# Attention and expert routing: the stretch ahead of the experts in a new order, and new clocks for where routing's steps go

## Chip, cores, metric

The kernel runs on one core of one Trainium2 chip. The metric is device time in microseconds (us) of one execution. The time before is the median of three runs, 891.27 us.

## The reference, cut to what matters

Sigmoid attention over 8 batches of 12 heads with 448 positions of width 64 gives x, 3584 tokens of width 768. A gate scores each token for 8 experts; a greedy assignment in order of score gives each expert exactly 448 tokens; each token goes through its expert's two products.

```python
attn = 1.0 / (1.0 + np.exp(-(scale * q @ k.T - np.log(S))))     # B,H,S,D = 8,12,448,64
x = (attn @ v).transpose(0, 2, 1, 3).reshape(B * S, H * D)      # 3584 x 768
logits = x @ w_gate                                             # 3584 x 8
for idx in np.argsort(-logits.flatten()):
    tok, e = idx // E, idx % E
    if assigned[tok] >= 0 or counts[e] >= cap: continue         # cap = 448
    assigned[tok] = e; counts[e] += 1
for e in range(E):
    m = assigned == e
    out[m] = np.maximum(x[m] @ w1[e], 0) @ w2[e]                # 768 -> 1024 -> 768
```

## The kernel before

The program's order is written by hand: each engine runs its instructions in the order in which the Python code emits them, and waits for data and buffers. An instruction that waits holds up everything behind it on its engine.

**Attention.** 48 pairs of heads, one after the other. `scores` makes products on TensorE and the sigmoid on ScalarE; `av` (L452 on) multiplies with v and copies the result from PSUM into `XT[b]` (six slots of 448 columns per batch) with VectorE (L469); for every second pair a rest is added to the slot before (L471). `logits(b, prs)` (L476 on) multiplies `XT` slots with the gate weights into `LE` (L482, L484). For the last batch, slots 0 to 3 go ahead of the last `av`, slots 4 and 5 behind it.

**Ahead of the experts.** `rows(b, c)` transposes 112 tokens of `XT` back (six TensorE transposes, L490), copies them with ScalarE into a buffer `xr` (L492) and writes them to `xs` in DRAM (L493, issued on SP's queue). There are 32 such row blocks, kept in the list `late`. `Router.start` transposes `LE` (L134) into `ML`, the table of scores. Then routing for the first expert runs on TensorE and VectorE; after each step that it yields, `LATE_PER_STEP` = 2 row blocks are emitted (`LATE_KEYS` after the first).

**Routing one expert** (`Router.phase`). `keys` (VectorE) makes a key per token and expert. `search` transposes the keys (L162, TensorE; copy L165, VectorE) and then finds the threshold of the 448th key for all experts in 16 steps: three counting instructions each (L173), a sum over partitions, and a few small ones. For expert 0 the sum is a TensorE product (L185); for the others it is done on VectorE alone. `pick` (L224 on) chooses the expert, `place` (L252, L257, L258) numbers its tokens, and `lists` compares the number's residue `rr` with 0 to 63 in one large VectorE instruction, the one-hot `oh` (L279), from which TensorE makes the list of tokens `idx` (L284, L291, L293).

**The experts.** `moe(kx)` is a generator that yields once per product of 448 columns: 144 for the first layer (L680 to L684, three per tile because each operand is split into a high and a low part) and 144 for the second (L715 to L719); 36 more for expert 0, whose first part is cut in two, and 48 more in the last. The loop at the end of the file drives it. It adds each product's cost (`MM` = 189 ns) to `clock[0]` and decides after each product what else to emit:

- a step of the next expert's routing, when the clock has passed `t_route`. The step yields the time (`T_KEYS`, `T_DVE`, ...) after which the next one follows, to which `SLACK` = 150 is added;
- a chore, at most one per `CHORE_NS` = 1000: the gather of a token block from `xs` (GpSimd's queue, L618), a *turn* of half a gathered block (`xturn`: three TensorE transposes L632 into a PSUM buffer `tp`, ScalarE's copy L635 to `xh`, VectorE's subtraction L636 to `xl`, which frees `tp`), or an `untranspose` of a part of the output (L645 into `tp`, copy L650). There are two `tp` buffers, used in turn. The chores of expert kx + 1 begin when its list is finished (`prepare`), the turns `lag` later.

`stream` loads weights through SP and splits them into `wh` (ScalarE, L596) and `wl` (L598, mostly GpSimd).

## Time and profile before

| | |
|---|---|
| runs | 888.68, 891.27, 891.42 us; median 891.27 |
| the profiled execution | 887.23 us; span from first to last instruction 885.5 us |
| mean granted TensorE clock | 0.984 |
| busy: TensorE, VectorE, ScalarE, GpSimd | 837.8, 531.4, 456.2, 467.4 us |
| attention | 0 to about 274 us of the span |
| ahead of the experts | about 274 to 335 us |
| experts | about 335 us to the end |

In a timeline row the numbers are start and length in us, then engine, line, operation, what it writes and reads, the shape, how many are merged, and in brackets the idle time of the engine before it with what ended it. A TensorE product's length is modelled and reaches beyond the start of the next one; the distance of two starts tells the pace.

### The profile page before, as it was taken

How to read it: one execution, taken by the hardware profiler on the slowest of the kernel's cores; microseconds unless marked ns; L12 is line 12 of the kernel's file. 1: busy time of each engine (PE TensorE's matmuls, PEld its weight loads, DVE VectorE, ACT ScalarE, POOL GpSimd, SP SyncE). 2: the span in 40 equal slices, each digit the busy share in tenths (PEclk: the TensorE clock that was granted, in tenths of full speed). 3: DMA queues.
4: the chain of work that ended last, by engine and by line, in shares of the span. 5: the costliest groups of instructions: out<-in, count | busy, mean ns of one | idle time of the engine just before them, and what ended most of it. 6: DMA issues, size and time to landing. Idle time of an engine off the chain costs nothing.

```text
span 885.5 us, 16232 instructions
## 1 busy us (share of the span) xinstructions
PE 837.8 (95%) x5507; PEld 639.0 (72%) x5507; DVE 531.4 (60%) x2047; ACT 456.2 (52%) x610; POOL 467.4 (53%) x449
## 2 busy tenths in 40 slices
PE   6999999999998729998999999999999999999996
PEld 3455455455555518987988988988888888889996
DVE  4665555555554778958869779779689521421110
ACT  6777777777774724434424424434434434443431
POOL 9645444444400014846864964873883882752651
PEclk9999999999999969999999999999999999999999
DMA  9876666665603945434443542452552542632511
GB/s 172 168 144 127 132 125 123 131 126 120 138 12 100 299 161 153 136 107 161 136 133 117 146 156 75 157 164 95 153 164 70 178 146 72 228 111 72 192 49 63
DMA packets 203507, 117.57 MB, mean 133 GB/s; under 512 B 143936, under 2 KB 193088, under 8 KB 203424
## 3 DMA queue, kind: packets, MB, share of 16 engines
q1 hardware_dynamic: 190688, 83.03, 36.0%
q0 software_dynamic: 10880, 33.28, 11.9%
q8 instruction: 43, 0.70, 0.3%
q10 hardware_dynamic: 1856, 0.23, 0.2%
q14 instruction: 40, 0.33, 0.1%
HBM read 94.47 MB, written 22.02 MB: 132 GB/s over the span
## 4 chain that ended last, share of the span: by engine, by line
PE 77%; DVE 8%; DMA 5%; issue 4%; POOL 3%; ACT 1%; SPq 1%; POOLq 0%; ACTq 0%; DVEq 0%
PE tp L461 13%; PE sc L437 11%; PE sc L682 8%; PE sc L680 8%; PE sc L684 8%; PE sc L717 6%; PE sc L719 6%; PE sc L715 6%; PE tp L467 2%; DMA xs<-xr 2%; DVE r_junk L173 2%; PE sc L447 2%; PE tp L645 2%; DMA xr<-xs,r_idx 2%; PE tp L632 2%
## 5 line engine op out<-in xcount | busy, mean ns | idle before, releaser
L598 POOL TENSOR_TENSOR wl<-wr,wh 128x768 fp32r<-128x768 f32 (+1 forms) x96 | 205.9, 2155 | 134.6 <-ACT wh L596 126.9
L427 ACT ACTIVATE at<-sc,bias 128x896 f32<-128x896 f32 x168 | 161.0, 1006 | 63.1 <-PE sc L447 38.2
L372 POOL DMA_DIRECT2D nkq<-in_q_dram x188 | 118.6, 646 | 111.5 <-DVE kqT L412 104.7
L719 PE MATMUL sc<-hh,wl 128*128 128x448 f32 (+2 forms) x400 | 151.4, 378 | 0.0
L717 PE MATMUL sc<-hl,wh 128*128 128x448 f32 (+2 forms) x400 | 145.4, 364 | 0.1
L684 PE MATMUL sc<-xh,wl 128*128 128x448 f32 (+2 forms) x396 | 145.4, 367 | 0.0
L682 PE MATMUL sc<-xl,wh 128*128 128x448 f32 (+2 forms) x396 | 144.9, 366 | 0.0
L715 PE MATMUL sc<-hh,wh 128*128 128x448 f32 (+2 forms) x400 | 143.9, 360 | 0.0
L680 PE MATMUL sc<-xh,wh 128*128 128x448 f32 (+2 forms) x396 | 143.8, 363 | 0.0
L173 DVE TENSOR_SCALAR_CACHE_REDUCE r_junk<-r_KE,r_T 128x224 bf16<-128x224 f32 x315 | 123.2, 441 | 0.1
L461 PE MATMUL tp<-at,nv 128*64 128x448 f32 x576 | 118.8, 548 | 0.0
L596 ACT ACTIVATE wh<-wr 128x768 fp32r<-128x768 f32 (+1 forms) x112 | 102.0, 939 | 13.2 <-DMA wr<-in_moe_w_dram 13.1
L692 POOL TENSOR_TENSOR hl<-yt,hh 128x896 fp32r<-128x896 f32 x32 | 68.3, 2136 | 44.5 <-ACT yt L691 41.8
L421 DVE TENSOR_TENSOR kqL<-kqT,kqH 128x896 fp32r<-128x896 f32 (+1 forms) x49 | 52.6, 1073 | 58.3 <-ACT kqH L419 58.2
L688 ACT ACTIVATE hh<-sc 128x896 fp32r<-128x896 f32 x32 | 29.5, 920 | 111.0 <-PE sc L684 111.0
L618 POOL DMA_INDIRECT xr<-xs,r_idx x32 | 32.0, 1002 | 97.5 <-ACT wh L596 86.7
L717 PEld LDWEIGHTS sc<-hl,wh 128*128 128x128 f32 x400 | 75.2, 188 | 7.0 <-issue 1.1
L598 DVE TENSOR_TENSOR wl<-wr,wh 128x768 fp32r<-128x768 f32 (+1 forms) x16 | 25.1, 1571 | 91.7 <-ACT wh L596 91.5
L461 PEld LDWEIGHTS tp<-at,nv 128*64 128x64 f32 x576 | 37.1, 136 | 59.1 <-issue 57.9
L682 PEld LDWEIGHTS sc<-xl,wh 128*128 128x128 f32 x396 | 74.5, 188 | 6.3 <-issue 0.5
L715 PEld LDWEIGHTS sc<-hh,wh 128*128 128x128 f32 x400 | 75.6, 189 | 4.4
L680 PEld LDWEIGHTS sc<-xh,wh 128*128 128x128 f32 x396 | 74.7, 189 | 5.5
(156 smaller groups left out, 1323.7 us busy)
## 6 DMA issues: line engine op xcount, KB each, us to landing
wr<-in_moe_w_dram SPq DMA_DIRECT2D x64, 384.0 KB
wr<-in_moe_w_dram SPq DMA_DIRECT2D x48, 512.0 KB
xs<-xr SPq DMA_DIRECT2D x32, 336.0 KB
nkq<-in_k_dram SPq DMA_DIRECT2D x190, 56.0 KB
nkq<-in_q_dram POOLq DMA_DIRECT2D x188, 56.0 KB, 2.6
nv<-in_v_dram SPq DMA_DIRECT2D x92, 96.0 KB
nr<-in_v_dram SPq DMA_DIRECT2D x46, 32.0 KB
xr<-xs,r_idx POOLq DMA_INDIRECT x32, 4.4
```

Source lines behind the costliest of these rows:

```text
L173: nc.vector.tensor_scalar(junk, KE, T[:, i:i + 1].bitcast(F32), None, OP.is_ge, OP.add, accum_out=cnt[:, i:i + 1])
L372: qn.dma_start(t[o:o + 32, n], rws[x])
L427: nc.scalar.activation(a, p[:, :, :S], AF.Sigmoid, bias=bias, scale=1 / math.sqrt(D))
L461: nc.tensor.matmul(p[j * 64:j * 64 + 64, :S], nat["v", b, g][:, h0 + j, c, :], AT[b, pr, c][:, j, :], start=(c == 0), stop=(c == 2 and pr ...
L596: nc.scalar.activation(hi, raw[u], AF.Copy)
L598: eng.tensor_tensor(lo, raw[u], hi.bitcast(F32), OP.subtract)
L680: nc.tensor.matmul(ph[:, f, lo:hi], wh[:, a, fs], xh[:, dd, lo:hi], start=st, stop=False)
L682: nc.tensor.matmul(ph[:, f, lo:hi], wh[:, a, fs], xl[:, dd, lo:hi], start=False, stop=False)
L684: nc.tensor.matmul(ph[:, f, lo:hi], wl[:, a, fs], xh[:, dd, lo:hi], start=False, stop=en)
L715: nc.tensor.matmul(py[:, d2, :w], wh[:, a, dsl], h1, start=st, stop=False)
L717: nc.tensor.matmul(py[:, d2, :w], wh[:, a, dsl], h2, start=False, stop=False)
L719: nc.tensor.matmul(py[:, d2, :w], wl[:, a, dsl], h1, start=False, stop=(j == 1 and a == 3))
```

## The change

It is made in four places.

1. *End of attention.* All six slots of the last batch's logits are made in one go after the loop; the last `XT` copy is made by ScalarE; no row block stands between the logits and `Router.start`.
2. *Ahead of the experts.* The pool with `XT` (`xa`) is opened below the attention's working pools `ld` and `wk`, which are closed first. In their space lie eight `xr` buffers (four before); the row blocks have three PSUM buffers (two before). The experts' PSUM pools `ps_t` and `ps_s` are opened after the row blocks, and the experts' SBUF pools now start on `XT`'s space. `LATE_KEYS` is 3.
3. *The one-hot's input.* For experts 1 to 7 the residue `rr` is written to PSUM as float32, not to SBUF as int16.
4. *The clocks.* `MM` is 206. A second clock `dve[0]` follows VectorE: a routing step adds its cost to it, a turn adds `T_XL`. The next step follows at `dve[0]` + `T_HOP` (150) if it begins on TensorE with what VectorE made, else at `dve[0]` + `T_FEED` (−400). Turns, untransposes and such TensorE beginnings now also advance `clock[0]` (`T_TURN`, `T_BACK`, `T_PE`). Step times are new, the sixteenth search step is emitted together with what follows it, and `lag` runs from 6500 to 17000 instead of 5000 to 14000.

```diff
-XA_BUFS = 4
+XO_BUFS = 8
-LATE_KEYS = 2
-T_KEYS, T_KE, T_STEP, T_DVE, T_KAP, T_PICK, T_TOT, T_OH, T_BT = 3600, 2100, 2050, 2025, 500, 2600, 600, 3800, 600
-SLACK = 150
+LATE_KEYS = 3
+T_KEYS, T_STEP0, T_STEP, T_KAP, T_PICK, T_TOT, T_OH, T_BT = 4850, 3300, 2340, 350, 3000, 700, 4900, 1500
+T_HOP, T_FEED, T_XL, T_TURN, T_BACK, T_PE = 150, -400, 560, 420, 300, 250
...
-            if not pe:
-                yield T_DVE
+            if not pe and st < 15:
+                yield T_STEP if st else T_STEP0, False
...
-        rr = wk.tile([112, 32], I16, name="r_rr")
+        rr = wk.tile([112, 32], I16, name="r_rr") if alone else P[:, 320:352]
...
-            yield T_KEYS
+            yield T_KEYS, True
             yield from self.search(k == 0)
-            yield T_KAP
+            yield T_STEP + T_KAP, True
...
-            nc.vector.tensor_copy(XT[b][:, pr, :], p[:, :S])
+            (nc.scalar.copy if (b, pr) == (B - 1, NP - 1) else nc.vector.tensor_copy)(XT[b][:, pr, :], p[:, :S])
...
-            if old == (B - 1, NP - 2):
-                bg.append(lambda: logits(B - 1, range(NP - 2)))
...
-        logits(B - 1, [NP - 2, NP - 1])
-        late.pop(0)()
+        logits(B - 1, range(NP))
...
         pctx.close()
-        ps_t = ctx.enter_context(tc.tile_pool(name="ps_t", bufs=2, space=PSUM))
-        ps_s = ctx.enter_context(tc.tile_pool(name="ps_s", bufs=2, space=PSUM))
+        lctx.close()
         ps_a = ctx.enter_context(tc.tile_pool(name="ps_a", bufs=2, space=PSUM))
+        xo = actx.enter_context(tc.tile_pool(name="xo", bufs=1))
+        ps_s = actx.enter_context(tc.tile_pool(name="ps_w", bufs=3, space=PSUM))
...
         actx.close()
+        ps_t = ctx.enter_context(tc.tile_pool(name="ps_t", bufs=2, space=PSUM))
+        ps_s = ctx.enter_context(tc.tile_pool(name="ps_s", bufs=2, space=PSUM))
...
 # in xturn:
+            if not wide:
+                clock[0] += T_TURN
+            dve[0] = max(dve[0], clock[0] + 900) + T_XL
...
 # in untranspose:
+            clock[0] += T_BACK
...
-        MM = 189
+        MM = 206
...
-                lag = max(5000, min(14000, start + 40000 - t0))
+                lag = max(6500, min(17000, start + 50000 - t0))
...
                 if t >= t_route:
-                    t_route = t + next(route, 0) + SLACK
+                    cost, hop = next(route, (0, False))
+                    dve[0] = max(dve[0], t) + cost
+                    clock[0] += T_PE if hopped[0] else 0
+                    hopped[0] = hop
+                    t_route = dve[0] + (T_HOP if hop else T_FEED)
```

## The prediction

> **What bounds the kernel now.** I read the page first, then the busy time by stretches, then the timelines of the stretch ahead of the experts and of one expert's turn into the next, then the list of waits.

> ```profile
> span 885.5 us, 16232 instructions
> PE 837.8 (95%) x5507; PEld 639.0 (72%) x5507; DVE 531.4 (60%) x2047; ACT 456.2 (52%) x610; POOL 467.4 (53%) x449
> ...
> 284.00:287.00 3.00, 1.88 (x17) 1.70 (x17) 2.45 (x17) 1.99 (x3) 0.00 (x0) 1.00 0.93 300
> ...
> 350.00:360.00 10.00, 10.00 (x51) 9.28 (x50) 9.44 (x61) 3.19 (x4) 8.42 (x6) 1.00 0.40 107
> ```

> Columns of a stretch: its length, busy time of PE, weight load, VectorE (DVE), ScalarE (ACT) and GpSimd (POOL), granted clock, DMA share, GB/s. TensorE is full except in two kinds of place. Ahead of the experts (274 to 335 us) it waits for VectorE, which runs the first of the searches, while the rows of x leave at 300 GB/s. From 335 us on it is full and VectorE nearly so while a search runs, so there the order of the two queues decides. The profiled execution took 887.23 us (its span and 1.8 around it), 4.0 less than the median 891.27; I sum differences and add them to the median. About 0.3%, 2.7 us, is what a measurement here can tell from no change.

> **Ahead of the experts.**

> ```profile
> 269.51 0.97 PE L482 MATMUL tp<-xt,wgz 128*32 128x112 f32 x32
> 270.42 2.48 PE L461 MATMUL tp<-at,nv 128*64 128x448 f32 x12
> 272.82 0.98 PE L467 MATMUL tp<-at,nr 64*64 64x448 f32 x8
> 275.18 0.59 PE L482 MATMUL tp<-xt,wgz 128*32 128x112 f32 x16 [1.37 <-DVE xt L471]
> 277.55 0.65 PE L134 MATMUL rt<-ident,LE 128*112 128x128 f32 x2 [0.98 <-ACT xr L492]
> ...
> 286.65 0.17 PE L185 MATMUL rt<-r_cnt,c_G 128*128 128x3 bf16 x1 [1.02 <-DVE r_junk L173]
> 288.50 0.16 PE L185 MATMUL rt<-r_cnt,c_G 128*128 128x3 bf16 x1 [0.32 <-DVE r_junk L173]
> 290.35 0.16 PE L185 MATMUL rt<-r_cnt,c_G 128*128 128x3 bf16 x1 [0.19 <-DVE r_junk L173]
> ...
> 316.85 0.16 PE L185 MATMUL rt<-r_cnt,c_G 128*128 128x3 bf16 x1 [1.68 <-DVE r_junk L173]
> ...
> 331.70 0.87 PE L632 MATMUL tp<-ident,xr 128*128 128x128 f32 x3 [5.05 <-DMA xr<-xs,r_idx]
> ...
> 273.88 0.62 DVE L469 COPY xt<-tp 128x448 f32<-128x448 f32 x1 [3.05 <-PE tp L467]
> ```

> (1) All 48 logit products of the last batch come after the last attention products, the first row block after R.start, and ScalarE makes the last XT copy. The 32 products at 269.51 leave the front: attention's end moves up 0.91 (270.42 − 269.51), from 273.8 to 272.9. The copy (0.62 on VectorE) runs beside VectorE's addition instead of ahead of it; both end at about 273.55. The logits' PSUM buffer is the one the copy frees, so the 48 start then, not earlier; 32 cost 0.91 and 16 cost 0.52, so they end at 275.0, not 275.7. LE's addition (0.27) follows, and L134 no longer waits for the row block's ScalarE copy: it starts at about 275.4, not 277.55. I take 2.2 us; bounds 0.7 (the logits alone) and 3.0.

> (2) Search 0 has 16 steps, with two row blocks behind each of the first 14. Undisturbed, a step takes 1.85 us (288.50 to 290.35). From 286.65 to 316.85 are 14 steps in 30.20, 2.16 each, because TensorE stands in front of a row block whose ScalarE copy waits:

> ```profile
> 305.19 1.60 ACT L492 COPY xr<-sc 112x768 f32<-112x768 f32 x2 [1.22 <-DMA xs<-xr]
> ...
> DMA to landing us min/median/max: 3.7/4.4/5.6
> ```

> Eight xr buffers and three of PSUM replace four and two. Will the DMA allow it? At 0.93 busy it moved 300 GB/s, 323 if full, so a block of 0.344 MB needs 1.07 to 1.15 us, against 0.925 asked: over 24 blocks it falls behind by 3.4 to 5.4 us, and four more buffers hold 4 × 1.1 = 4.4. It just about fits. So 14 × (2.16 − 1.85) = 4.3 us; bounds 0 (DMA sets the pace after all) and 4.3.

> The three early row blocks (LATE_KEYS 3) replace the one that stood ahead of R.start: 32 either way. The rest of the chain, pick to first gather, is the same instructions. Moving xa below ld and wk puts the weight buffers on XT's space; they must wait for the last row block on TensorE, and the two search steps left after it (3.7 us) and the pick cover that. The writes to xs end at about 278 + 32 × 1.1 + 2 = 315; the gathers that read them start one landing (4.4) ahead of the first turn, at 331.7 − 4.4 − 6.5 = 321. On SP's queue the first weights stand behind the same 32 writes. This costs nothing, at most 1 us where the weights meet the last writes.

> Ahead of the experts: −6.5 us (−0.7 to −7.5).

> **In the experts.** I counted the emission in both versions, matmul by matmul, with the code's own clocks. The plain pace is 25 matmuls in 5.06 us, 0.2025 each, so MM 189 ran 7% fast and 206 is right.

> ```profile
> 373.83 0.36 PE L719 MATMUL sc<-hh,wl 128*128 128x448 f32 x1
> ...
> 378.89 0.36 PE L715 MATMUL sc<-hh,wh 128*128 128x448 f32 x1
> ...
> 461.18 0.39 PE L162 MATMUL rt<-ident,r_KT 112*128 112x112 f32 x2
> 463.26 0.49 PE L632 MATMUL tp<-ident,xr 128*128 128x128 f32 x3
> 464.81 0.49 PE L632 MATMUL tp<-ident,xr 128*128 128x128 f32 x3
> ...
> 468.72 0.55 PE L632 MATMUL tp<-ident,xr 128*128 128x128 f32 x3 [0.65 <-DVE xl L636]
> ...
> 475.23 0.39 PE L632 MATMUL tp<-ident,xr 64*128 64x64 f32 x3 [0.15 <-DVE xl L636]
> ...
> 463.79 0.49 ACT L635 ACTIVATE xh<-tp 128x384 fp32r<-128x384 f32 x1 [0.32 <-PE tp L632]
> ...
> 461.60 0.39 DVE L165 COPY r_KE<-rt 128x224 f32<-128x224 f32 x1 [0.57 <-PE rt L162]
> ...
> 465.33 0.55 DVE L636 TENSOR_TENSOR xl<-tp,xh 128x384 fp32r<-128x384 f32 x1
> ...
> 468.12 1.01 DVE L636 TENSOR_TENSOR xl<-tp,xh 128x384 fp32r<-128x384 f32 x2
> ...
> 471.38 1.01 DVE L636 TENSOR_TENSOR xl<-tp,xh 128x384 fp32r<-128x384 f32 x2
> ```

> A turn (xturn) needs one of two tp buffers, and the turn two before frees it with VectorE's subtraction L636. If a search step was emitted in between, that subtraction stands behind 2.3 us of VectorE work (468.12 − 465.83; a pair of subtractions takes 1.01). That is the wait at 468.72: TensorE stops, and all its matmuls queue behind the turn.

> Before, turns are 6 matmuls apart (6 × 189 passes CHORE_NS = 1000) and steps 12. Now T_TURN adds 420 to the clock, so 3 × 206 + 420 already passes 1000: turns are 3 matmuls apart. T_XL charges VectorE's clock, but t_route was set when the last step was issued, so the charge moves the next step but one. In expert 1 the count, in matmul numbers: first step (with L162) 246, turns 251, 254, step 255, turns 257, 260, 263, step 265, turns 266, 269, 272. Before: first step 239, turns 248 to 288, four steps in between.

> TensorE from L162 to the last turn, after: 26 × 0.2025 + 7 turns × 0.33 (464.81 − 463.26 less 6 matmuls) + L162 0.26 (461.18 to 463.26 less 9 matmuls) = 7.8 us. VectorE until that turn may start (it needs the sixth subtraction): 0.42 to the key copy, 3.5 for copy and first step (461.60 to 465.33, less some 0.2 that the step lost to POOL's splits), two subtractions 1.0, a step 2.3, two 1.0, 0.6 idle because the fifth turn starts only when the third's buffer is free (0.53 to ScalarE, 0.49 there), 0.55, a step 2.3, 0.5: 12.1 in round numbers. TensorE stands 4.3 us; I take 4.0. The same sum for before: 49 × 0.2025 + 2.3 + 0.26 = 12.5 against 0.42 + 3.5 + 6 × 0.5 + 3 × 2.3 = 13.8, a wait of 1.3; the trace has 14.05 from 461.18 to 475.23, so 1.5. The method holds.

> (3) Experts 1 to 4 turn their successors among search steps; in 5 and 6 the searches are over. After: 4 × 4.0 = 16. Before, this row bounds it:

> ```profile
> PE tp L632 <- DVE xl L636: 3.2, 5, 0.9
> ...
> 405.49 1.01 PE L632 MATMUL tp<-ident,xr 128*128 128x128 f32 x6 [0.85 <-DVE xl L636]
> ...
> 407.21 0.86 PE L632 MATMUL tp<-ident,xr 64*128 64x64 f32 x6 [0.71 <-DVE xl L636]
> ```

> 3.2 less 1.56 at the first turn of experts is 1.6; the brackets leave out some 0.2 to 0.3 of modelled tail at each stall, so I take 3.5. Difference +12.5; bounds 0 (the steps fall clear of the turns) and +14.4.

> (4) Expert 0 to 1: the list is finished at matmul 288 (281 before), the last three gathers stay behind the weight split on POOL, and a search step now falls between the third turn and its predecessors. +1; bounds 0 and +2.5.

> (5) T_KEYS 4850 puts 26 matmuls (5.3 us) instead of 20 (4.1) between the keys and their transposes. T_OH 4900 gives the one-hot 24 instead of 21. Those waits go:

> ```profile
> 648.34 0.38 PE L162 MATMUL rt<-ident,r_KT 112*128 112x112 f32 x2 [0.31 <-DVE r_KT L153]
> ...
> 516.64 1.08 PE L284 MATMUL rt<-r_oh,c_mv 112*32 112x64 f16 x32 [0.28 <-DVE r_oh L279]
> ```

> Four of the first kind (one each for experts 2 to 5) and one of the second: −1.5.

> (6) The residue in PSUM:

> ```profile
> L279 DVE TENSOR_TENSOR r_oh<-c_io,r_rr x8: 1215/1440/3005, 323.7 to 712.7; 112x2048 f16<-112x2048 int16 x8
> ...
> 448.75 0.19 PE L257 MATMUL rt<-r_mk,c_TRI 112*112 112x64 bf16 x1
> ...
> 451.15 3.00 DVE L279 TENSOR_TENSOR r_oh<-c_io,r_rr 112x2048 f16<-112x2048 int16 x1
> ```

> No row has this comparison with an f32 input from PSUM. Operations that do read PSUM in f32 take 0.55 us for 384 elements (465.33) and 0.62 for 448 (273.88), 1.1 ns an element, so 2048 take 2.4. It starts 2.4 after L257 (448.75 to 451.15), 4.8 in all under 24 matmuls, 4.9: hidden, cost nothing. At the 3.00 of the slowest row it would cost 0.5 seven times, 3.5; at the fastest, 1.22, nothing again, and a gain has no way in once TensorE does not wait.

> Everything else in the clocks (T_BACK, T_PE, T_PICK, T_BT, lag) moves work among full TensorE time: nothing.

> Sum in the experts: 12.5 + 1 − 1.5 = +12. Whole: 12 − 6.5 = +5.5, so 891.3 + 5.5 = **897 us**; its own range is 892 to 902.

> **A rule weighed: the clock.**

> ```profile
> 274.00:278.00 4.00, 1.84 (x25) 1.49 (x26) 1.30 (x4) 0.80 (x1) 0.00 (x0) 0.93 0.00 0
> 278.00:281.00 3.00, 3.00 (x16) 2.92 (x15) 2.53 (x6) 1.01 (x2) 0.00 (x0) 0.52 0.39 120
> ...
> 400.00:410.00 10.00, 6.88 (x42) 5.28 (x41) 7.58 (x31) 4.91 (x10) 2.96 (x4) 1.00 0.42 139
> ```

> With TensorE 46% busy over 4 us the clock was halved for 3.4 us behind it; with 69% over 10 us it was not. My stalls of 1.3 to 1.6 us lie between turns and leave TensorE over half busy, so I add nothing; were all four groups and the first turn to halve the clock, 5 × 3.4 / 2 = 8.5 us come on top. [...]

> **The rivals.** *Faster, by the search steps clearing the turns.* If VectorE reaches the subtractions as T_XL means it to, the groups' waits go (−3.5), with +1, −1.5 and −6.5: 891.3 − 10.5 = 881; with some left, 881 to 886. It decides from the point where a group stands less than 2.6 us ((6.5 + 1.5 + 3.5 − 1) / 4). For it speaks the new pace of TensorE's clock; against it the 2.3 us between pairs of subtractions. 0.17.

> *About level:* groups at half my wait: 891 − 2.5 = 889, up to 893. 0.12.

> *The change ahead of the experts does not do what it says:* the writes were 0.93 busy already, so the pace stays 2.16 and only 2.2 is won: 891.3 + 12 − 2.2 = 901. Against it: only 4 blocks in flight at 4.4 us each. 0.08.

> *The clock falls in the stalls:* 897 + 1.7 to 8.5 = 899 to 905. 0.06.

> My forecast has 0.57.

> **How the numbers follow.** Faster than 888.6 holds the first rival and part of the second: 0.20. Within 2.7 us: the rest of the second and the low end of mine: 0.13. Slower: 0.67. The range 884 to 903 leaves out the lower part of the first rival (about 0.1) and the clock's upper part.

> **What would show it.** In the trace after: L185 steps 1.85 apart with no ScalarE wait for xs; L134 near 275.4; first turn of expert 0 near 325, not 331.7; in the waits, L632 for L636 at 12 us or more with three stalls per expert 1 to 4, each behind a search step; no wait at L162; L279 near 2.3. I am wrong if the turns' stalls stay under 2 us an expert, or the writes hold the first search.

## The result, and the profile after

The changed kernel takes **903.63 us** (median; 902.76 to 904.55), the kernel before 891.27: ratio **1.0146 [1.0125, 1.0168]**, 12.4 us slower. The forecast was 897 (884 to 903). Slow executions, one of before (2087.74 us) and one of e2 (954.11 us), are left out of all medians. The profiled execution of after took 904.55 us, 17.3 more than the one of before (887.23), so the differences of the two traces add up to 17.3, not 12.4.

Of a timeline only the rows that are read are shown. Line numbers are those of each kernel's own file: in after a turn's transposes are L636 and its subtraction L640, in before they are L632 and L636. A turn group is the eight turns of one expert's blocks; it is named after the expert among whose products it stands.

The page of after, first lines:

```profile
span 902.8 us, 16228 instructions
PE 842.9 (93%) x5507; PEld 644.1 (71%) x5507; DVE 529.1 (59%) x2045; ACT 455.9 (51%) x611; POOL 464.8 (51%) x449
```

TensorE runs the same 5507 matmuls and is 5 us busier: part of its work ran at a lower clock (mean granted 0.978, before 0.984). The rest of the 17.3 us it stood.

TensorE's timeline of after, ahead of the experts (start, length, line; in brackets the idle time and its end):

```profile
275.53 0.40 PE L134 MATMUL rt<-ident,LE 128*112 128x128 f32 x2 [0.49 <-DVE csum L125]
281.83 0.16 PE L185 MATMUL rt<-r_cnt,c_G 128*128 128x3 bf16 x1 [0.51 <-DVE r_junk L173]
284.38 0.16 PE L185 MATMUL rt<-r_cnt,c_G 128*128 128x3 bf16 x1 [1.01 <-DVE r_junk L173]
...
310.23 0.16 PE L185 MATMUL rt<-r_cnt,c_G 128*128 128x3 bf16 x1 [1.68 <-DVE r_junk L173]
325.94 0.87 PE L636 MATMUL tp<-ident,xr 128*128 128x128 f32 x3 [5.90 <-DMA xr<-xs,r_idx]
```

This stage came out as forecast: L134 at 275.53 instead of 277.55, and from 284.38 to 310.23 are 14 steps of 1.85. The last L185 is 6.6 us earlier; at the first expert product 6.1 are left. So the experts cost 6.1 + 17.3 = 23.4 us more. By expert (distance of first products, us):

| expert | 0 | 1 | 2 | 3 | 4 | 5 | 6 | 7 |
|---|---|---|---|---|---|---|---|---|
| before | 72.71 | 67.53 | 68.72 | 68.06 | 67.74 | 69.45 | 64.57 | 71.37 |
| after | 74.99 | 74.13 | 73.27 | 71.10 | 72.47 | 69.29 | 66.17 | 72.15 |
| difference | +2.3 | +6.6 | +4.6 | +3.0 | +4.7 | −0.2 | +1.6 | +0.8 |

First TensorE, then VectorE in the turn group of expert 1, after:

```profile
463.43 0.36 PE L722 MATMUL sc<-hl,wh 128*128 128x448 f32 x1
464.64 0.55 PE L636 MATMUL tp<-ident,xr 128*128 128x128 f32 x3 [0.85 <-DVE xl L640]
...
466.38 0.36 PE L722 MATMUL sc<-hl,wh 128*128 128x448 f32 x1
467.89 0.55 PE L636 MATMUL tp<-ident,xr 128*128 128x128 f32 x3 [1.15 <-DVE xl L640]
...
472.40 0.40 PE L636 MATMUL tp<-ident,xr 64*128 64x64 f32 x3 [1.28 <-DVE xl L640]
...
474.46 0.57 PE L720 MATMUL sc<-hh,wh 128*128 128x448 f32 x1
474.83 0.57 PE L722 MATMUL sc<-hl,wh 128*128 128x448 f32 x1
```

```profile
464.03 1.02 DVE L640 TENSOR_TENSOR xl<-tp,xh 128x384 fp32r<-128x384 f32 x2
464.96 0.44 DVE L173 TENSOR_SCALAR_CACHE_REDUCE r_junk<-r_KE,r_T 128x224 bf16<-128x224 f32 x1
...
467.17 0.21 DVE L212 TENSOR_SCALAR r_J<-r_acc,r_J 128x1 int32<-128x1 int32 x1
467.29 1.01 DVE L640 TENSOR_TENSOR xl<-tp,xh 128x384 fp32r<-128x384 f32 x2
```

A pair of subtractions, a whole search step (464.96 to 467.29), the next pair. The turn at 467.89 needs the first of the second pair. It starts 1.51 us behind the product ahead of it (466.38) in place of some 0.2, so TensorE stands 1.3. The bracket shows less than that, because a product's modelled end lies behind the next start. Turns and steps came in the order of the forecast. The waits, after:

```profile
PE tp L636 <- DVE xl L640: 16.7, 12, 3.3
```

before: 3.2 us in 5 waits. Right behind the group, at 474.46 and 474.83, products are 0.37 apart, not 0.20: that is the clock. Windows of after, most of them 3.41 us long and cut where the clock changes (length; busy time of PE, weight load, VectorE, ScalarE, GpSimd; granted clock; DMA share; GB/s):

```profile
398.07:401.49 3.42, 1.19 (x9) 0.94 (x9) 3.28 (x17) 1.68 (x3) 0.00 (x0) 1.00 0.16 49
401.49:404.90 3.41, 2.82 (x13) 1.87 (x12) 1.77 (x5) 1.91 (x5) 0.00 (x0) 0.50 0.00 0
404.90:408.31 3.41, 3.41 (x13) 3.00 (x12) 3.27 (x20) 1.22 (x3) 2.70 (x3) 0.50 0.01 2
455.00:480.00 25.00, 21.72 (x112) 18.25 (x111) 21.06 (x100) 8.85 (x17) 8.06 (x7) 0.93 0.32 104
463.00:473.00 10.00, 6.72 (x39) 4.92 (x38) 8.46 (x42) 3.58 (x8) 2.73 (x2) 1.00 0.22 66
469.75:473.17 3.42, 2.13 (x13) 1.44 (x12) 2.72 (x16) 0.99 (x3) 1.82 (x1) 1.00 0.17 27
473.17:476.58 3.41, 3.41 (x13) 2.89 (x12) 3.24 (x20) 0.71 (x2) 0.00 (x0) 0.50 0.27 96
531.19:534.60 3.41, 0.51 (x4) 0.51 (x5) 3.27 (x17) 0.00 (x0) 0.00 (x0) 1.00 0.39 118
534.60:538.02 3.42, 3.42 (x14) 2.62 (x12) 3.02 (x16) 0.98 (x2) 0.00 (x0) 0.50 0.00 0
602.86:606.27 3.41, 1.70 (x11) 1.23 (x10) 3.27 (x19) 0.97 (x2) 0.09 (x1) 1.00 0.35 115
665.00:690.00 25.00, 21.89 (x117) 18.52 (x115) 21.93 (x127) 10.99 (x22) 8.42 (x4) 0.93 0.22 69
674.55:677.97 3.42, 1.94 (x12) 1.18 (x11) 2.42 (x13) 1.57 (x4) 2.17 (x1) 1.00 0.00 0
677.97:681.38 3.41, 3.41 (x12) 2.90 (x13) 2.97 (x18) 0.65 (x2) 0.20 (x1) 0.50 0.37 115
```

The stretches that start at 398.07, 469.75, 531.19 and 674.55 leave TensorE idle for a third to five sixths, and each is followed by one at 0.50, in which some 13 matmuls run in place of 20. (The one at 401.49 leads into a second one.) These are five stretches, 17.1 us, in the experts; in the trace of before there is none from 0.2 us into them on, but for the last 4 us, where both traces have one. TensorE stood for 0.6 of it (2.82 busy of 3.41) and does half the work in the rest: (17.1 − 0.6) / 2 = **8.2 us** lost, 1.1 of it in expert 0, 7.1 in experts 1, 2 and 4. Without it experts 1 to 4 are 18.9 − 7.1 = 11.8 us longer: the turns' stalls. Expert 3 has the stalls and no half clock (602.86).

The 8.2 us are counted against one execution of before. Not every execution of before is as free of half clock: of 32 that ran beside the experiments, the 13 with a mean granted clock of 0.984 or more took 888.9 us on average, the 13 with 0.981 or less 891.5. And e1, whose part for the experts is that of before, has a half-clock stretch in its trace from 402.21 to 405.62, behind the change from expert 0 to 1. So some of the 8.2 is missing from the difference of the medians; how much is not shown, since the execution of 887.23 us is the only one of before with a trace.

**Expert 6** is 1.6 us longer for a reason that the forecast did not have. TensorE, then GpSimd (POOL), after:

```profile
780.35 0.37 PE L687 MATMUL sc<-xl,wh 128*128 128x448 f32 x1
782.17 0.47 PE L689 MATMUL sc<-xh,wl 128*128 128x448 f32 x1 [1.45 <-POOL wl L599]
```

```profile
774.73 0.99 POOL L619 DMA_INDIRECT xr<-xs,r_idx  x1 [0.30 <-issue]
...
778.22 2.13 POOL L697 TENSOR_TENSOR hl<-yt,hh 128x896 fp32r<-128x896 f32 x1
780.30 1.81 POOL L599 TENSOR_TENSOR wl<-wr,wh 128x768 fp32r<-128x768 f32 x1
```

With the new `MM` the gathers for expert 7 come after products 24, 29 and 34 of expert 6 instead of 32, 38 and 44. Three of them, 3.5 us from 774.73 to 778.22, stand ahead of the weight split on GpSimd's queue, and a product waits for that split. The traces of e2 to e7, all with this `MM`, have the same stall of 1.6 to 1.8 us; e1, with the old one, has not.

### The profile page after: what moved, and what is told of

The parts are those of the page before. It is cut to its first block, busy times and chain, and to the rows that moved or that the text cites. A ratio compares the mean times of both kernels' runs of the same rounds, so it can differ in the third digit from the quotient of the medians.

```text
span 902.8 us, 16228 instructions
## 1 busy us (share of the span) xinstructions
PE 842.9 (93%) x5507; PEld 644.1 (71%) x5507; DVE 529.1 (59%) x2045; ACT 455.9 (51%) x611; POOL 464.8 (51%) x449
## 4 chain that ended last, share of the span: by engine, by line
PE 78%; DVE 12%; issue 5%; POOL 3%; DMA 1%; ACT 1%; ACTq 0%; SPq 0%; POOLq 0%; DVEq 0%
PE tp L462 13%; PE sc L438 11%; PE sc L689 8%; PE sc L685 8%; PE sc L687 8%; PE sc L724 6%; PE sc L720 6%; PE sc L722 6%; DVE r_junk L173 5%; PE tp L468 2%; PE sc L448 2%; PE tp L650 2%; PE tp L636 1%; DVE xl L640 1%; PE tp L483 1%
## 5 line engine op out<-in xcount | busy, mean ns | idle before, releaser
L722 PE MATMUL sc<-hl,wh 128*128 128x448 f32 (+2 forms) x400 | 148.4, 371 | 0.2 <-POOL hl L697 0.2
L720 PE MATMUL sc<-hh,wh 128*128 128x448 f32 (+2 forms) x400 | 147.6, 369 | 0.0
L685 PE MATMUL sc<-xh,wh 128*128 128x448 f32 (+2 forms) x396 | 145.8, 368 | 0.0
L173 DVE TENSOR_SCALAR_CACHE_REDUCE r_junk<-r_KE,r_T 128x224 bf16<-128x224 f32 x315 | 123.3, 442 | 0.1
L597 ACT ACTIVATE wh<-wr 128x768 fp32r<-128x768 f32 (+1 forms) x112 | 101.6, 938 | 14.1 <-DVE r_oh L279 11.3
L599 DVE TENSOR_TENSOR wl<-wr,wh 128x768 fp32r<-128x768 f32 (+1 forms) x16 | 18.6, 1168 | 107.4 <-ACT wh L597 107.4
L689 PEld LDWEIGHTS sc<-xh,wl 128*128 128x128 f32 x396 | 74.9, 189 | 7.8 <-POOL wl L599 1.8
L724 PEld LDWEIGHTS sc<-hh,wl 128*128 128x128 f32 x400 | 76.4, 191 | 5.6 <-issue 0.7
```

The source lines that it names most:

```text
L173: nc.vector.tensor_scalar(junk, KE, T[:, i:i + 1].bitcast(F32), None, OP.is_ge, OP.add, accum_out=cnt[:, i:i + 1])
L597: nc.scalar.activation(hi, raw[u], AF.Copy)
L599: eng.tensor_tensor(lo, raw[u], hi.bitcast(F32), OP.subtract)
L685: nc.tensor.matmul(ph[:, f, lo:hi], wh[:, a, fs], xh[:, dd, lo:hi], start=st, stop=False)
L689: nc.tensor.matmul(ph[:, f, lo:hi], wl[:, a, fs], xh[:, dd, lo:hi], start=False, stop=en)
L720: nc.tensor.matmul(py[:, d2, :w], wh[:, a, dsl], h1, start=st, stop=False)
```

## The experiments

Ratios are to runs of the kernel before on the same chip (890.31 us for e1 to e4, 891.10 for e5 to e8). They can differ a little from the quotient of the medians.

| kernel | us | ratio [95%] |
|---|---|---|
| e1: before + parts 1, 2 | 882.80 | 0.9925 [0.9906, 0.9944] |
| e6: before + parts 3, 4 | 909.15 | 1.0209 [1.0189, 1.0229] |
| e4: after without part 3 | 903.93 | 1.0162 [1.0143, 1.0181] |
| e2: after, turns 6 products apart | 892.23 | 1.0027 [1.0013, 1.0040] |
| e3: after, no step between turns | 892.09 | 1.0043 [1.0019, 1.0068] |
| e5: after, the stalls filled with products | 904.71 | 1.0152 [1.0129, 1.0176] |
| e7: e3, steps held earlier | 885.04 | 0.9941 [0.9924, 0.9959] |
| e8: before, turns 3 products apart | 902.41 | 1.0127 [1.0105, 1.0150] |

**e1: the stretch ahead of the experts alone.** Parts 1 and 2 of the diff on the kernel before; the old clocks and `rr` in SBUF.

> The kernel before with only parts 1 and 2 of the change (end of attention, row blocks); clocks and one-hot as before. Theory A (the loss is made in the experts, by search steps between turns and by the clock that falls in those stalls; the stretch ahead gains by itself): last L185 near 310.2, first turn near 326, experts as long as before, 891.3 - 6 = 885 us. Rival B (the new order ahead of the experts also shifts what follows, its weights and gathers meeting the writes): 890 us or more, with the experts longer than 550 us.

882.80, −7.5 us. Its timeline of TensorE:

```profile
281.92 0.16 PE L185 MATMUL rt<-r_cnt,c_G 128*128 128x3 bf16 x1 [0.51 <-DVE r_junk L173]
...
310.30 0.16 PE L185 MATMUL rt<-r_cnt,c_G 128*128 128x3 bf16 x1 [1.68 <-DVE r_junk L173]
...
326.06 0.66 PE L633 MATMUL tp<-ident,xr 128*128 128x128 f32 x2 [5.93 <-DMA xr<-xs,r_idx]
```

The same places as in after within 0.15 us. The gain of this half is real and nothing gives it back. Of the kernels run this is the fastest, ahead of before and of after.

**e6: the experts' part alone**, parts 3 and 4 on the kernel before.

> The kernel before with only parts 3 and 4 of the change (one-hot, clocks). Theory A (the two halves of the change add up): 890.3 + 13.3 + 7.5 = 911 us, experts as long as in the changed kernel within 3 us. Rival B (the loss in the experts comes with the new pools and order ahead of them): 890 to 900 us.

909.15, +18.1 us. With e1's −7.5 that is +10.5, against +12.4 for both: the halves nearly add. So the whole loss belongs to parts 3 and 4.

**e4: the one-hot's input back in SBUF.**

```diff
-        rr = wk.tile([112, 32], I16, name="r_rr") if alone else P[:, 320:352]
+        rr = wk.tile([112, 32], I16, name="r_rr")
```

> The changed kernel with the residue back in SBUF as int16 for all experts (part 3 undone). Theory A: the one-hot is hidden either way; L279 takes 1.22 to 3.0 us instead of 2.28, the time is 903.6 within 2 us. Rival C (the one-hot in PSUM makes VectorE late for the turns): 3 us or more faster, group stalls at least 1 us shorter each.

903.93, as after. All instructions of L279, after:

```profile
L279 DVE TENSOR_TENSOR r_oh<-c_io,rt x7: 2277/2277/2277, 382.2 to 722.3; 112x2048 f16<-112x2048 int16 x7
L279 DVE TENSOR_TENSOR r_oh<-c_io,r_rr x1: 1216/1216/1216, 317.1 to 317.1; 112x2048 f16<-112x2048 int16 x1
```

With PSUM it takes 2.28 us, 1.06 more than the undisturbed one from SBUF, and no product waits for it after expert 0. Part 3 costs nothing and brings nothing; the loss is the clocks' (part 4).

**e2: more products between turns.** A turn sets the next chore 1600 ahead instead of 1000, so turns are again 6 products apart; all else as in after.

```diff
+                gap[0] = TURN_NS                        # in a turn; TURN_NS = 1600
-                        t_chore = t + CHORE_NS
+                        t_chore, gap[0] = t + gap[0], CHORE_NS
```

> The changed kernel with one thing altered: after a turn the next chore comes 1600 clock units later, not 1000, so turns stand 6 matmuls apart as before. Theory A: each pair of turns has a search step's length on TensorE, the stalls of the four groups fall from about 16.7 us in all to 4, the clock halves at most at the first change of experts: 903.6 - 12 - 5 = 886 to 888 us. Rival C (the loss comes from the step times and the PSUM one-hot, not from the distance of turns): 901 to 904 us.

892.23: some 11 us of the 12 come back, not the 16 or more that I expected. The waits of L636's line fell from 16.7 to 9.7 us:

```profile
PE tp L637 <- DVE xl L641: 9.7, 8, 3.2
```

The groups of experts 1 to 3 keep no stall above 1.2 us and no half clock. One stall of 3.4 us in expert 4 and the change from expert 0 to 1 remain, with half clock around both (665.1 to 668.5, 398.8 to 409.1). The stall in expert 4 follows a VectorE instruction (L206) that took 2.79 us in place of 0.23 (650.35 to 653.14): from there to the subtraction that the turn waits for, at 664.83, VectorE runs steps without a pause. The last section comes back to L206. Against e1 (882.80) 9 us are still lost, so the distance of the turns is not the whole of it.

**e3: no search step between turns.** From a group's first turn to its last no routing step is emitted.

```diff
+                busy[0] = (j, hf) != (3, 1)             # in a turn
-                if t >= t_route:
+                if t >= t_route and not busy[0]:
```

> The changed kernel with one thing altered: from the first to the last turn of a group no search step is emitted; turns stay 3 matmuls apart. Theory A: without a step between them the turns run as in experts 5 and 6 of the changed kernel, 0.94 us apart with no stall; group stalls about 2 us in all, no halved clock in the groups, routing some 5 us later per expert: 885 to 890 us. Rival D (turns 3 apart are too close for ScalarE and VectorE whatever lies between): 898 to 904 us.

892.09, 2 us above what I expected; its ten executions reach from 889.76 to 899.02, and the trace is of the fastest. TensorE's turns in the groups of experts 1 and 4:

```profile
458.51 0.49 PE L637 MATMUL tp<-ident,xr 128*128 128x128 f32 x3
459.45 0.49 PE L637 MATMUL tp<-ident,xr 128*128 128x128 f32 x3
461.82 0.55 PE L637 MATMUL tp<-ident,xr 128*128 128x128 f32 x3 [1.27 <-DVE xl L641]
...
664.20 0.90 PE L637 MATMUL tp<-ident,xr 128*128 128x128 f32 x3 [2.75 <-DVE xl L641]
```

Turns with no step between them follow at 0.94 and do not wait (458.51, 459.45). What is left in these two groups is at the third turn: steps emitted ahead of the first turn still lie on VectorE's queue. (In expert 2 the first turn waits for its gather, 1.8 us at 527.33.) VectorE runs behind TensorE when a group begins, which the order of emission alone does not show.

**e7: the same, with the steps held sooner.** Steps stop 1500 of the clock's ns ahead of the first turn, until the last.

```diff
+                quiet[0] = t0 + lag - LEAD              # LEAD = 1500
-                if t >= t_route:
+                if t >= t_route and (quiet[0] is None or t < quiet[0]):
```

> As e3_hold, but search steps are held back from 1500 clock units ahead of a group's first turn until its last. Theory A (what is left of e3_hold's stalls, one of 1.2 to 2.9 us at the third turn of each group, is steps already in VectorE's queue): these stalls fall under 1 us each, no clock halved among the groups: 892 - 6 = 886 us, about 4 us above e1_ahead for expert 6's weight split and the slower products. Rival D (the pair of buffers or ScalarE limits turns 3 apart): 890 us or more, the stalls as in e3_hold.

885.04, as expected (886): the steps are the same, only their place moved. Windows over its groups in experts 1 and 3:

```profile
455.00:480.00 25.00, 24.64 (x140) 21.20 (x139) 16.81 (x68) 11.79 (x23) 14.58 (x16) 1.00 0.44 152
...
595.00:620.00 25.00, 24.05 (x136) 21.00 (x135) 17.68 (x91) 12.16 (x23) 14.46 (x16) 1.00 0.41 144
```

TensorE is all but full and the clock 1.00 in these and in the other two; the only half clock left between the first 1.2 us of the experts and their end is 401.4 to 404.9. With the stalls the clock's loss is gone too, and the experts' part costs some 2 us against e1 instead of 21.

**e8: the distance alone.** The kernel before, with its old clocks, and turns 3 products apart (the e2 edit with 500).

> The kernel before with one thing altered: after a turn the next chore comes 500 clock units later, not 1000, so turns stand 3 matmuls apart; clocks, step times and one-hot as before. Theory A (the distance of turns among search steps makes the stalls, whatever the clocks): 2 to 3 us more in each of experts 1 to 4, 890.3 + 8 to 13 with what the clock loses = 898 to 903 us. Rival C (it takes the new step times): 888 to 892 us.

902.41, +11.3 us, as expected. A part of the group of expert 2, windows of e8:

```profile
530.00:537.50 7.50, 5.39 (x30) 4.28 (x29) 6.93 (x32) 1.47 (x3) 5.09 (x4) 1.00 0.68 235
537.50:540.90 3.40, 3.06 (x11) 2.78 (x12) 1.30 (x3) 0.85 (x2) 0.00 (x0) 0.50 0.01 4
```

Moving the turns together, which is what `T_TURN` does to them, is enough for 11 of the 18 us that the new clocks cost in e6, half clock included. The other 7 come with the rest of the new clocks; no run takes these apart.

**e5: are the stalls time in which TensorE could work, and does the clock follow?** In the groups of experts 1 to 4, 2 to 6 products whose sums go unused stand ahead of five of the eight turns, 20 a group, 80 in all; at 0.2025 that is 16.2 us of work.

> The changed kernel with 20 extra products of 448 columns put ahead of the waiting turns in each of the four groups (4, 2, 6, 2, 6 of them; their sums are used by nothing): 80 products, 16.2 us of TensorE work at 0.2025 us each. Theory A (TensorE stands there for VectorE, and its clock falls because it stands): the extra products run inside the stalls, cost 4 us at most, and the clock no longer halves in the groups (5 us less): 898 to 904 us. Rival E (TensorE's own work sets the time in these stretches; the clock falls by itself): 903.6 + 16 = 920 us, halved stretches as before.

904.71 against 903.63, 0.7 above the range that I expected: 16.2 us of added work cost 1. Windows of e5 over the groups of experts 1 and 4:

```profile
455.00:480.00 25.00, 24.98 (x138) 21.78 (x138) 20.38 (x96) 9.18 (x18) 8.93 (x8) 1.00 0.32 104
665.00:690.00 25.00, 24.51 (x135) 21.43 (x136) 20.72 (x119) 9.83 (x19) 10.49 (x5) 1.00 0.22 64
```

After had 21.72 and 21.89 busy there, and 0.93 granted. In both the half clock is gone where TensorE was given work, with VectorE as busy as ever; at 534.7, where a stall of 2.7 us stayed, it is still there. So in these groups it fell because TensorE stood, not because of what VectorE or the turns did. By the two traces experts 1 to 4 together are 1.3 us longer than in after, with 7.6 us less of half clock, which is worth 3.8; by that some 5 of the 16.2 lay on the path, and 11 in time when TensorE stood.

## Why the prediction was wrong in size

Direction and mechanism were right, the time was 6.6 us short. By its steps:

- **(1) and (2)**, ahead of the experts: −6.5 forecast, −6.6 at the last L185, −6.1 at the first expert product, −7.5 by e1. The DMA allowed 1.85 per step, as the 4.4 us of buffer against 3.4 to 5.4 had said.
- **(3)** and **(5)**, turns and waits: 16 us of turns' waits forecast; 16.7 are listed, 13.9 of them in the four groups. From the distances of starts, TensorE stands 15.3 us in the four groups. That the sum fits so well is in part luck: the forecast had three stalls in each group, and only expert 1 has three (1.0 to 1.5 us), the others two each (1.3 to 1.9 us, and one of 3.5). Of that one some 2.1 us come from the held L206 (last section), which the forecast did not have. Experts 1 to 4 without the clock: +11.8 against 12.5 − 1.5 = 11.0. e8 and e2 show the distance as a cause, e3 and e7 the steps between.
- **(4)**, the change of experts 0 and 1: +1 forecast; expert 0 is 2.3 longer, 1.1 of it clock.
- **(6)**: 2.28 us instead of 2.4, hidden, shown by e4.
- **The step that failed is "A rule weighed: the clock", at "so I add nothing".** Between the two traces it measured 8.2 us, close to the 8.5 that the same paragraph named as the most. The rival with the fallen clock, to which I gave 6 in 100, came true together with the forecast's mechanism.
- **Not in the forecast at all:** expert 6's wait for a weight split (+1.6) and a slower pace of products in expert 7 (+0.8). I had counted emission for the turns and steps, not for the gathers against GpSimd's queue, which went under "moves work among full TensorE time: nothing".

Of the 17.3 us between the two traces −6.1, +11.8, +1.2 and −0.2 are forecast terms (6.7 against 5.5), the clock 8.2, expert 6 1.6, expert 7 0.8. The two traces are 4.9 us further apart than the medians, so what was left out adds up to more than the 6.6 by which the forecast was short.

Two things were wrong in the paragraph on the clock. I set a row of 10 us (400 to 410 of before, 69% busy, no half clock) against my stalls. Over 10 us the row 463 to 473 of after is 67% busy as well, and the clock fell behind it. The changes of clock lie on a grid of 3.41 us (last section), and in the stretch from 469.75 on, the one ahead of the fall, TensorE was 62% busy by the row and worked 46% by the count given there. And that stalls which leave TensorE over half busy cost no clock was my estimate: the two rows showed a fall at 46% busy and none at 69%, and nothing between. A window that is only a little more than half idle, 54% by that count, was enough at 469.75.

## What to carry to other kernels

A stall of TensorE had two prices here: its own length, and, where it left 53% or more of a 3.41 us window idle, in 8 of 26 windows up to 69% and in all 31 above that, also half clock behind it: some 1.7 us lost in each full stretch of 3.41 us at a granted 0.50. Weigh both when stalls come in groups. When work is placed by modelled clocks, spreading the turns by buffer releases (or keeping the other queue's long step away from them) can matter more than exact clocks: here the new clocks moved the turns closer together, and the experts' part cost 18 us (e6); with the steps held away from the turns (e7) the same clocks cost some 2. Count each queue that a changed clock feeds, GpSimd's too.

## What the runs showed of the hardware

**VectorE held by GpSimd.** One row of VectorE, then one of GpSimd, in the group of expert 2, after:

```profile
528.80 2.33 DVE L206 TENSOR_SCALAR r_T<-c_kk,r_J 128x3 int32<-128x3 int32 x1
```

```profile
528.70 2.39 POOL L599 TENSOR_TENSOR wl<-wr,wh 128x1024 fp32r<-128x1024 f32 x1
```

L206 works on three elements and takes 0.23 us in five of seven cases; here 2.33, and it ends within 0.04 us of GpSimd's split. It lies ahead of the longest stall of all: the turn at 534.10 starts 3.7 us behind the product ahead of it. The row is no exception. From 325 us on this instruction (L206, in e5 and e7 L207) runs 60 times in the ten traces. All 23 that begin while GpSimd has more than 0.13 us left of a subtraction take 0.62 to 2.79 us and end within 0.04 us of the end of one; the 37 others take 0.23. L191, the same operation on the same tile but written to PSUM, keeps 0.18 to 0.19 us in all its 840 runs, beside such work too. The one-hot L279 of experts 1 to 7 is alike: 1.22 to 3.43 us in 28 cases with its inputs in SBUF, 2.28 in all 42 with one in PSUM. By what means GpSimd's work holds up VectorE's is not shown.

**Two paces of the same product.** In after, products of the first layer of expert 7 start 206.4 ns apart, in before 202.6, both at clock 1.00; stretches of the slower pace also lie in experts 1, 4, 5 and 6 of after and in other kernels, with the old clocks too (e8, 348 to 383 us). The one in expert 6 ends at the stall at 780.35. The cause is open; no run tests it.
